# Loads of q and k in half-size transfers and short packets, in a fused window attention and highway layer

## The chip, the core and the metric

The kernel runs on one core of one Trainium2 chip. Five engines work side by side, each through its own instructions in order: PE (TensorE: matmuls, and transposes against an identity matrix), DVE (VectorE), ACT (ScalarE), POOL (GpSimd) and SP (SyncE, which here only issues DMAs). Sixteen DMA engines move data between HBM and the core's SBUF. They take their work from queues: one is fed by POOL, another by SP. The metric is the device time of one execution in microseconds (us), lower is better. The profile is one further execution; its span runs from the first to the last instruction, and the device time of that same execution is a little longer than its span.

## What is computed

```python
B, H, S, D = 8, 8, 576, 64          # q, k, v: [B, H, S, D], float32
scores = scale * q @ k.T            # per batch and head
mask   = (rel >= 0) & (rel < 128)   # rel = query position - key position
attn   = softmax(where(mask, scores - slope[h] * abs(rel), -1e9))
x      = (attn @ v)                 # heads side by side: [4608, 512]
h      = maximum(x @ w_h, 0)
t      = sigmoid(x @ w_t + b_t)
out    = t * h + (1 - t) * x        # [4608, 512], float32
```

Each query sees the 128 keys that end with its own, so that only a band of the scores is worked out. Eight slopes, one for each head, weight the distance.

## The kernel before

**Tiling.** The kernel works on 8 batches. A batch of q or k is 8 heads of 576 positions of 64 numbers. In SBUF it lies as 128 partitions x 2 halves x 1152 bf16: a half is four heads (a = 0 or 1), and a partition holds, for each half, 18 positions of one head, which are 1152 numbers that lie together in HBM: 4608 bytes of float32. The DMA turns float32 into bf16 on its way, so a row arrives as 2304 bytes. The output is worked out in 36 blocks of 128 rows: four to a batch, and one more for each pair of batches from their last 64 rows.

**The steps.** The order of all work is written out by hand as one long string, ORDER; every letter is one step, and each engine gets its instructions in the order of the string. The letters that matter here:

- L, a load, issued by POOL. The list LOADS gives their order: the four halves of q and k of batch 0 into buffers of their own (hq, hk), v of batch 0, the two weight matrices (wH, wT), the bias, then q, k and v of the other batches (lq, lk, va). There are 29 loads: 4 halves, 14 whole q or k, 8 of v and 3 of weights and bias. A v load takes 64 numbers a time, 36 for each partition.
- S, pieces of set-up: on POOL an index (iota, L245) and the identity matrix (ident, L276); on DVE a cast of the index (kq, L253), small operands (kb, ex), 0/1 masks (m, L263 and L265) and their products with the slopes (mk, L268).
- T, a transpose of one half of q or k by DVE into tq or tk (L290), 32 of them. It reads hq, hk, lq or lk.
- s, e, m: scores on PE (L311), their exponential on ACT (p, L326), the mask on DVE (p times mk, both in SBUF, L336).
- V: a copy of half of v's rows to other partitions (vb), by DVE for batches 0 to 2 (L209) and by DMAs of SP for the others (L211).
- p, n: attention times v on PE (L356); DVE divides and writes x (L366, L367).
- x, c, h, r, z, b, a, t: transpose of x on PE against ident (L382), copies and activations on ACT, the two matrix products on PE (L392, L425).
- u, g, o, d: DVE subtracts x (uu, L402 or L404) and multiplies by the gate (uu, L445); the last addition (ot, L450) is done by POOL for 29 of the 36 blocks and by DVE for the others; SP stores the block (L456, L460).

**Buffers.** lq and lk have three buffers each, va and vb four, x eight, uu and ot six each. A load that is issued must find its buffer free.

**What sets the order around the change.** POOL does its loads, its two pieces of set-up and its additions in one sequence. Up to its second addition that is: the four halves, v0, wH, wT, the bias, the index, q1, k1, v1, q3, ident, q2, v2, k2, k3, v3, the first addition, q4, k4, the second addition. The waits are put in by the framework that the kernel is written in, not by the kernel's author.

Of the kernel before, what the change touches and what calls it, by code (L numbers as in the profile page):

```python
# [121 lines left out]
def kernel(  # L122
# [10 lines left out]
    nc = tc.nc  # L133
# [47 lines left out]
    def load(kind, b=0, a=None):  # L181
        if kind in "qk":
            src = (q if kind == "q" else k)[b].rearrange(
                "(a g) (s t) d -> (g s) a (t d)", a=2, t=18)
            if a is None:
                dst = (LQ if kind == "q" else LK)[b % NL]
                nc.gpsimd.dma_start(out=dst[:], in_=src)
            else:
                dst = (HQ if kind == "q" else HK)[a]
                nc.gpsimd.dma_start(out=dst[:], in_=src[:, a])  # L190
        elif kind == "v":
            nc.gpsimd.dma_start(  # L192
                out=VA[b % NV][:, :, 0:D],
                in_=v[b].rearrange("h s d -> (h s) d").rearrange("(c p) d -> p c d", p=P))
        elif kind in "HT":
            i = "HT".index(kind)
            nc.gpsimd.dma_start(
                out=(wH, wT)[i][:],
                in_=(moe_w_h, moe_w_t)[i].rearrange("(c p) n -> p c n", p=P))
        else:  # L200
            nc.gpsimd.dma_start(
                out=bT[0:1, :], in_=moe_b_t.rearrange("(o n) -> o n", o=1))
# [249 lines left out]
    def store(b, s):  # L452
# [5 lines left out]
        for half in range(2):  # L458
            row = (2 * b + half) * S + 512
            nc.sync.dma_start(out=out[row : row + D, :], in_=ot[half * D : (half + 1) * D, :])  # L460

    do = dict(S=setup, L=load, V=move, T=tr, s=scores, e=soft, m=mask, p=pv, n=norm, x=x_tr, c=x_copy, h=mm_h,
              r=relu_act, u=relu_sub, b=bias, B=spread, C=spread_copy, z=mm_z, a=tanh, t=to_gate, g=gate, o=add_x, d=store)
    by = lists()
# [36 lines left out]
```

## Time and profile before

| | us |
|---|---|
| median of three runs | 162.2 |
| lowest and highest of them | 161.84, 163.52 |
| the profiled execution, device time | 161.35 |
| the profiled execution, span | 159.6 |

In the views below, a row of a timeline or of the chain begins with the start in us from the start of the span and the duration in us. A group of instructions has its line, engine, operation, what it writes and reads, its count, and then busy time in us, the mean of one in ns, and the idle time of the engine just before them. "DMA packets" counts what the DMA engines moved in a window, with the size as it is written and GB/s as written. A row of the DMA view for one issue ends with the time from issue to landing in us. The line of 40 digits is the busy share of the DMA engines in 40 equal slices of the span, in tenths.

### The profile page before, as it was taken

The numbers are of one execution on the slowest core, as the hardware profiler recorded it, in microseconds if no ns is written. First come the engines' busy times: TensorE is split into PE (matmuls) and PEld (weight loads), VectorE is DVE, ScalarE is ACT, GpSimd is POOL, SyncE is SP. The second block draws the span as 40 slices with busy tenths as digits, with TensorE's granted clock in tenths as the row PEclk, the third lists the DMA queues.
The fourth block names the chain that finished last, engine by engine and source line by source line (L and its number), as shares of the span: only waits on it lengthen the run. The fifth ranks groups of instructions, "written<-read, shape, count | busy, mean of one in ns | idle before, by whom it ended". The sixth has DMA issues, their size and how long they took to land.

```text
span 159.6 us, 6226 instructions
## 1 busy us (share of the span) xinstructions
PE 131.2 (82%) x2695; PEld 75.3 (47%) x2695; DVE 143.6 (90%) x309; ACT 123.4 (77%) x209; POOL 66.2 (41%) x65
## 2 busy tenths in 40 slices
PE   0003989879998997899999888999999999999940
PEld 0002774345545443555565455555654655656410
DVE  6698879999999999999998999999999999998770
ACT  3001966699878797988989998978989899998740
POOL 7993624562447845422239451354041302210220
PEclk9999999999999999999999999999999999999995
DMA  3999999999999999999999999943103132321333
GB/s 42 193 168 188 209 208 167 201 211 197 250 208 198 253 255 230 214 215 189 252 275 195 178 208 217 282 104 130 66 4 136 68 102 55 116 72 70 131 119 79
DMA packets 48540, 26.55 MB, mean 166 GB/s; under 512 B 38144, under 2 KB 39168, under 8 KB 48512
## 3 DMA queue, kind: packets, MB, share of 16 engines
q0 software_dynamic: 42464, 15.21, 84.2%
q1 hardware_dynamic: 6048, 10.94, 20.3%
q8 instruction: 21, 0.34, 0.9%
q14 instruction: 7, 0.06, 0.1%
HBM read 30.41 MB, written 9.44 MB: 250 GB/s over the span
## 4 chain that ended last, share of the span: by engine, by line
PE 50%; DVE 31%; ACT 8%; issue 5%; DMA 3%; POOL 0%; DVEq 0%; POOLq 0%
PE fs L392 14%; PE fs L425 9%; PE ps L356 9%; PE ps L311 8%; DVE tk L290 6%; DVE x L367 5%; DVE p L336 5%; DVE tq L290 4%; ACT p L326 4%; PE fs L382 3%; DMA hq<-in_q_dram 3%; DVE uu L445 3%; PE ps L425 3%; DVE uu L402 2%; DVE vb L209 2%
## 5 line engine op out<-in xcount | busy, mean ns | idle before, releaser
L450 POOL TENSOR_TENSOR ot<-uu,x 128x512 f32<-128x512 bf16 x29 | 36.0, 1245 | 69.0 <-DVE uu L445 41.1
L326 ACT ACTIVATE p<-ps 128x768 bf16<-128x768 f32 x64 | 49.9, 826 | 7.4 <-PE ps L311 7.4
L311 PE MATMUL ps<-tq,tk 32*64 32x192 bf16 (+2 forms) x1152 | 28.7, 251 | 16.4 <-DVE tk L290 14.3
L336 DVE TENSOR_TENSOR p<-p,mk 128x768 bf16<-128x768 bf16 x64 | 36.4, 590 | 2.1 <-ACT p L326 1.4
L392 PE MATMUL fs<-wH,xt 128*128 128x512 bf16 x140 | 36.1, 381 | 1.7 <-ACT xt L387 1.3
L311 PEld LDWEIGHTS <-tk 32*64 32x64 bf16 x1152 | 20.2, 110 | 24.8 <-DVE tk L290 14.8
L367 DVE TENSOR_TENSOR x<-ps,rd 128x512 bf16<-128x512 f32 x36 | 24.9, 692 | 2.0 <-DVE rd L366 0.5
L425 PE MATMUL fs<-wT,xt 128*128 128x512 bf16 x104 | 26.6, 380 | 0.0
L356 PE MATMUL ps<-va,p 64*128 64x65 bf16 (+1 forms) x544 | 23.5, 194 | 0.9 <-issue 0.4
L356 PEld LDWEIGHTS <-p 64*128 64x128 bf16 (+1 forms) x1088 | 19.1, 98 | 9.9 <-issue 7.1
L433 ACT ACTIVATE tt<-fs 128x512 f16<-128x512 f32 x26 | 15.9, 610 | 7.2 <-PE fs L429 4.8
L356 PE MATMUL ps<-vb,p 64*128 64x65 bf16 (+1 forms) x544 | 21.1, 193 | 0.0
L397 ACT ACTIVATE hh<-fs 128x512 bf16<-128x512 f32 x29 | 17.6, 605 | 3.6 <-PE fs L392 3.3
L425 PEld LDWEIGHTS <-xt 128*128 128x128 bf16 x144 | 12.8, 98 | 14.0 <-issue 0.5
L387 ACT COPY xt<-fs 128x512 bf16<-128x512 bf16 x30 | 17.7, 590 | 1.3 <-PE fs L382 1.2
L392 PEld LDWEIGHTS <-xt 128*128 128x128 bf16 x144 | 11.7, 98 | 14.7 <-ACT xt L387 3.9
L290 DVE STREAM_TRANSPOSE tk<-lk 128x576 uint32<-128x576 uint32 x14 | 17.3, 1246 | 0.0
L290 DVE STREAM_TRANSPOSE tq<-lq 128x576 uint32<-128x576 uint32 x14 | 17.2, 1244 | 0.0
L192 POOL DMA_DIRECT2D va<-in_v_dram x8 | 14.7, 1838 | 5.6 <-DVE p L336 4.8
L438 ACT ACTIVATE tt<-tt 128x512 f16<-128x512 f16 x25 | 16.0, 641 | 0.4
L445 DVE TENSOR_TENSOR uu<-uu,tt 128x512 bf16<-128x512 bf16 x36 | 14.9, 419 | 0.3
L382 PE MATMUL fs<-ident,x 128*128 128x128 bf16 x120 | 12.4, 226 | 3.4 <-DVE x L367 3.0
(55 smaller groups left out, 121.1 us busy)
## 6 DMA issues: line engine op xcount, KB each, us to landing
out_dram<-ot SPq DMA_DIRECT2D x32, 256.0 KB, 4.2
va<-in_v_dram POOLq DMA_DIRECT2D x8, 576.0 KB, 21.1
lq<-in_q_dram POOLq DMA_DIRECT2D x7, 576.0 KB, 20.0
lk<-in_k_dram POOLq DMA_DIRECT2D x7, 576.0 KB, 18.1
vb<-va SPq DMA_DIRECT2D x10, 146.2 KB, 7.0
out_dram<-ot SPq DMA_DIRECT2D x8, 128.0 KB, 4.5
hq<-in_q_dram POOLq DMA_DIRECT2D x2, 288.0 KB, 4.6
hk<-in_k_dram POOLq DMA_DIRECT2D x2, 288.0 KB, 6.3
```

The costliest lines, as they stand in the source:

```text
L290: nc.vector.transpose(out=u32(dst[b % NT][:, a].rearrange("p s e -> p (s e)")).rearrange("p (s t) -> p t s", t=18), in_=u32(src).rearrange ...
L311: nc.tensor.matmul(out=sc[j * D : (j + 1) * D, r, off : off + n * D], lhsT=KT[rows, j, t * D : (t + 1) * D, e], rhs=QT[rows, j, t * D : (t ...
L326: nc.scalar.activation(out=pview(i), in_=SC.pop((b, s, x))[:, :, 0:384].rearrange("p r (g n) -> p r g n", g=2), func=ACTF.Exp, scale=scale)
L336: nc.vector.tensor_tensor(out=p, in0=p, in1=mk, op=ALU.mult)
L356: nc.tensor.matmul(out=av[orow, j, hh * (D + 1) : (hh + 1) * (D + 1)], lhsT=PB[PT[bb, ps, x]][rows, r, lo : lo + orow.stop - orow.start], ...
L367: nc.vector.tensor_tensor(out=x[:], in0=av[:, :, :, 0:D], in1=rd[:].to_broadcast([P, 2, 4, D]), op=ALU.mult)
L387: nc.scalar.copy(out=xt[:], in_=XP.pop(at))
L392: nc.tensor.matmul(out=pa, lhsT=XT[at][:, c * P : (c + 1) * P], rhs=wH[:, c, :], start=c == 0, stop=c == NC - 1)
L397: nc.scalar.activation(out=hh[:], in_=PA.pop(at), func=ACTF.Relu)
L425: nc.tensor.matmul(out=PZ[at], lhsT=xt[:, c * P : (c + 1) * P], rhs=wT[:, c, :], start=own and c == 0, stop=not own and c == NC - 1, skip_ ...
L445: nc.vector.tensor_tensor(out=uu[:], in0=uu[:], in1=TT.pop(at)[:], op=ALU.mult)
L450: eng.tensor_tensor(out=ot[:], in0=UU.pop(at)[:], in1=xf(at), op=ALU.add)
```

## The change

Each whole load of q or k becomes two loads, one for each half of four heads, issued one right after the other from the same place in the order. All q and k loads, the four half loads of batch 0 too, get an upper limit on the length of a packet: 1152 bytes as read, in place of the whole row of 4608, so that a row goes in four packets, each 576 bytes as written. The number of loads grows from 29 to 43. Their order, the buffers, the loads of v and of the weights, and all other steps stay as they are.

```diff
             if a is None:
                 dst = (LQ if kind == "q" else LK)[b % NL]
-                nc.gpsimd.dma_start(out=dst[:], in_=src)
+                for half in range(2):
+                    nc.gpsimd.dma_start(out=dst[:, half], in_=src[:, half],
+                                        max_dma_last_dim=1152)
             else:
                 dst = (HQ if kind == "q" else HK)[a]
-                nc.gpsimd.dma_start(out=dst[:], in_=src[:, a])
+                nc.gpsimd.dma_start(out=dst[:], in_=src[:, a], max_dma_last_dim=1152)
```

## Prediction

> **What bounds the kernel now.** I read the page first, then the chain of work that ended last in its order of time, the timeline of POOL, the DMA view in short windows, and last the timeline of DVE beside POOL's.
>
> ```profile
> span 159.6 us, 6226 instructions
> ...
> PE 131.2 (82%) x2695; PEld 75.3 (47%) x2695; DVE 143.6 (90%) x309; ACT 123.4 (77%) x209; POOL 66.2 (41%) x65
> ...
> DMA  3999999999999999999999999943103132321333
> ...
> L290 DVE STREAM_TRANSPOSE tk<-lk 128x576 uint32<-128x576 uint32 x14 | 17.3, 1246 | 0.0
> L290 DVE STREAM_TRANSPOSE tq<-lq 128x576 uint32<-128x576 uint32 x14 | 17.2, 1244 | 0.0
> ```
>
> The DMA engines are full for two thirds of the span, which looks like a bound, but the last number of the two transpose groups says otherwise: DVE never stood idle for a whole q or k load. What ends last is seen in the chain:
>
> ```profile
> 6.99 1.26 DVE tq L290
> 8.25 0.04 DVE kq L253
> ...
> 8.87 1.17 DVE tk L290
> 10.04 1.21 DVE m L263
> 14.33 0.88 PE ps L311 x29
> ...
> 20.76 0.54 PE fs L382 x4
> ...
> 29.73 0.69 DVE uu L404
> ...
> 67.43 0.40 PE fs L382 x4
> ```
>
> DVE's set-up carries it to 14.33 us, PE and ACT to 29.7, DVE to 67.4, then mostly PE. Between 29.7 and 67.4 a microsecond lost on DVE is close to a microsecond of the kernel.
>
> **The change, part by part.** *POOL's issuing.* All loads are issued by POOL, in order with its own arithmetic:
>
> ```profile
> 1.32 1.25 POOL L190 DMA_DIRECT2D hq<-in_q_dram  x2 [0.81 <-POOLq L485]
> ...
> 3.61 1.86 POOL L192 DMA_DIRECT2D va<-in_v_dram  x1
> 5.42 0.80 POOL L197 DMA_DIRECT2D wH<-in_moe_w_h_dram  x1
> 6.17 0.79 POOL L197 DMA_DIRECT2D wT<-in_moe_w_t_dram  x1
> ...
> 7.52 0.48 POOL L245 IOTA kq_i<- 64x64 int32 x2
> 7.95 0.73 POOL L187 DMA_DIRECT2D lq<-in_q_dram  x1
> ...
> 9.38 1.86 POOL L192 DMA_DIRECT2D va<-in_v_dram  x1
> 11.20 0.73 POOL L187 DMA_DIRECT2D lq<-in_q_dram  x1
> 11.99 0.44 POOL L276 TENSOR_SCALAR_AFFINE_SELECT ident<-ident 128x128 bf16<-128x128 bf16 x1
> 14.72 0.85 POOL L187 DMA_DIRECT2D lq<-in_q_dram  x1 [2.28 <-DMA va<-in_v_dram]
> ```
>
> A transfer of 128 x 4 pieces is what wH and wT are already: one each 0.75 us (5.42 to 6.17). So each of the 14 whole loads costs POOL 2 x 0.75 in place of 0.73, some 0.8 us more, 11 us in all; the four half loads at the start go from 2.29 us together (1.32 to 3.61) to about 3.2 (four of 0.75, the first 0.2 longer as it is now), 0.9 more.
>
> *In flight.* The thirteenth load (14.72) goes into a buffer that nothing has used and yet waits for the fifth, va. So a load waits for the one eight places ahead, and 14 more loads make eight places hold less: a q or k fills two. That, not POOL's 11 us, moves things.
>
> ```profile
> va<-in_v_dram POOLq DMA_DIRECT2D x1, 576.0 KB, 10.8
> wT<-in_moe_w_t_dram POOLq DMA_DIRECT2D x1, 512.0 KB, 12.8
> lq<-in_q_dram POOLq DMA_DIRECT2D x1, 576.0 KB, 15.3
> lk<-in_k_dram POOLq DMA_DIRECT2D x1, 576.0 KB, 25.1
> ```
>
> These are the issues at 3.61, 6.17, 7.95 and 19.28, with the time to landing last: 14.4, 19.0, 23.3 and 44.4 us. The DMA queue always has work, so landings depend on the rate, not on when POOL issued; even so few places hold more than 10 us of transfers. But POOL stands still until a place comes free.
>
> *The rate.* Packets of 576 bytes as written (1152 as read) stand in no row; these windows have the neighbours, 2304, 128 and 1024 bytes:
>
> ```profile
> DMA packets 388, 0.81 MB, mean 202 GB/s; under 512 B 37, under 2 KB 37, under 8 KB 388
> ...
> DMA packets 3646, 0.48 MB, mean 161 GB/s; under 512 B 3628, under 2 KB 3646, under 8 KB 3646
> ...
> DMA packets 621, 0.62 MB, mean 207 GB/s; under 512 B 25, under 2 KB 617, under 8 KB 620
> ```
>
> (5 to 9, 10 to 13 and 15 to 18 us.) On 16 engines a packet starts every 12.7 ns at 128 bytes and every 79 at 1024; halfway is 46 ns, 201 GB/s. A whole load of 590 KB takes 2.92 us at 202 GB/s, 2.93 at 201, 3.66 at 161, 2.85 at 207: from -0.07 to +0.74 us a load, and I take 0, as the near rows are the large ones. There is room for some: k of batch 2 lands at 44.4, its second half is read at 47.0, so 2.6 us. With 2 loads' worth of half loads, q1, k1, q3, q2 and k2 ahead, that is 0.37 us a load.
>
> The Trainium skill, DMA: Bandwidth & Descriptors, How a descriptor splits into AXI transactions, speaks against this: reads go in pieces of 256 bytes from aligned addresses, and 1152 is 4.5 of them, so by it every second packet starts unaligned, and a row takes 152 beats in place of 144. By that a load is estimated at 2.92 x 152/144 = 3.08 us, and the sum would be some 0.3 us higher, from the start alone.
>
> *The start.* POOL's index iota ends 0.9 us later, at 8.9. DVE's cast of it ended at 8.28, right behind tq; now it ends at 9.1, and tk ends at 10.85. On the other side the two m operations, 1.21 us on the chain and now over at 11.25, ended with the v load that POOL was issuing (9.38 + 1.86 = 11.24). That load is now the thirteenth and waits for va's 14.4. m then meets half loads of 0.75 us: free at once it is over at 10.95, held to the end of one at 11.1, of the next at 11.85. So PE's start moves by -0.3 to +0.6 us; I take -0.1. The ident of L276 was ready at 12.43; ahead of it are now both halves of q3, the second waiting for wT: 19.2 with the later first packet, 0.3 from landing to issue (14.4 to 14.72), 0.75, then 0.5 for the select: 20.75, where PE reads it at 20.76. Bound: 0.5 later if the wait is slower. I take +0.1 for both together.
>
> *The adds.* v3, the last load ahead of the first add of POOL (L450), becomes the twenty-third and waits for the second half of q3, at 11.20 + 21.5 = 32.7:
>
> ```profile
> lq<-in_q_dram POOLq DMA_DIRECT2D x1, 576.0 KB, 21.5
> ...
> 27.95 1.41 POOL L450 TENSOR_TENSOR ot<-uu,x 128x512 f32<-128x512 bf16 x1 [2.29 <-DVE uu L445]
> ...
> 32.85 1.33 POOL L450 TENSOR_TENSOR ot<-uu,x 128x512 f32<-128x512 bf16 x1
> ```
>
> So the first add goes to 34.9 us from 27.95. Both halves of q4 and k4 follow; the second half of k4 waits for k2's first half, about 42.9, so the second add goes from 32.85 to about 44. From there POOL catches up, near 60. Buffers do not bite: uu has six, and the first add's is needed by the seventh subtraction at 48.45 (row below). Stores go late with the adds, harmless by the same count.
>
> What the adds do to DVE is the largest term:
>
> ```profile
> 32.70 1.80 DVE L209 COPY vb<-va 64x1170 bf16<-64x1170 bf16 x2
> 34.54 0.56 DVE L336 TENSOR_TENSOR p<-p,mk 128x768 bf16<-128x768 bf16 x1
> ...
> 48.45 0.40 DVE L402 TENSOR_TENSOR uu<-hh,x 128x512 bf16<-128x512 bf16 x1
> ...
> L336 DVE TENSOR_TENSOR p<-p,mk 128x768 bf16<-128x768 bf16 x14 | 9.3, 688 | 0.1
> L402 DVE TENSOR_TENSOR uu<-hh,x 128x512 bf16<-128x512 bf16 x8 | 3.8, 476 | 0.0
> L209 DVE COPY vb<-va 64x1170 bf16<-64x1170 bf16 x4 | 3.3, 834 | 0.1
> ...
> L209 DVE COPY vb<-va x6: 461/464/1305, 14.5 to 50.8; 64x1170 bf16<-64x1170 bf16 x6
> ```
>
> (The groups are DVE's from 30 to 66 us, the last line the copies of the whole run with their shortest, median and longest in ns.) The second copy of 32.70 ends only after the add of 32.85 has (34.18): a DVE operation on two SBUF tiles, or a copy, that starts while an add runs waits for its end. Against 0.56, 0.40 and 0.46 us undisturbed, the groups lose 14 x 0.13 + 8 x 0.08 + 4 x 0.37 = 3.9 us to nine adds, 0.43 each. An add that is not released by the DVE operation ahead of it comes at any moment: of DVE's 63 operations in this stage 36 are of those kinds, they start at 1.75 per us, so an add of 1.25 us catches one in about 7 of 10 cases, with some 0.7 us left: 0.5 each. Ten adds then fall in the stage, o0 among them: 5.0 us, +1.1.
>
> *Nothing else.* DVE's 14 more landings to wait for are all past; PE, ACT and the stores have the same work.
>
> **Sum:** +0.1 start, 0 rate, +1.1 adds: +1.2. On the profiled execution's 161.35 us (span 159.6) that is 162.55; that one was 0.85 under the median of 162.2, so 163.4 us.
>
> **The rivals.** *Hidden:* the late adds catch as much as the punctual ones did ; only the start counts, 162.3 us. For it: POOL has 59% of its time idle. *Faster:* the late adds fall behind transposes, which do not wait. At 0.15 us each that is 10 x 0.15 - 3.9 = -2.4, 159.9 us; it is faster by 1% once the mean is under 0.22 us. Against it: 36 of 63 operations do wait. *Pile-up:* the second to fifth adds queue up on POOL with nothing between them, and DVE loses each time what it loses now without cover, 0.85 us at 32.70 (1.80 for two copies of 0.46): 4 x 0.85 + 6 x 0.5 - 3.9 = +2.5, 164.8 us; it is slower by 1% once the mean of all ten is over 0.54 us. *Slow packets:* at 161 GB/s seven loads bring k2's second half 5.2 us late, 2.6 beyond its room: 163.4 + 2.6 = 166.0 us. Against it: the 1024-byte row is as fast as the large packets. The rule on alignment alone gives 163.7 and lies within the forecast.
>
> **How the numbers follow.** Forecast (162.8 to 164.1) 0.42, hidden 0.20, faster 0.16, pile-up 0.14, slow packets 0.08. The range runs from 160.6, inside the faster case, to 165.6, inside the last two; it leaves out about 0.2. About 1%, 1.6 us, is what a measurement of this kernel can tell from no change. Faster by more: most of the faster case, 0.14. Slower by more, above 163.8: pile-up, slow packets and a quarter of the forecast, 0.14 + 0.08 + 0.11 = 0.33. Within: 0.53.
>
> **What would show it.** POOL's issues of half loads at 0.75 us; the first add near 35 and the second near 44 us; ident near 20.7 and PE's first read of it near 20.9; DVE's m free of the v load; windows of q or k packets near 200 GB/s; the p, uu and vb groups from 30 to 66 us 5 us over undisturbed. I am wrong if loads do not wait for a place (adds on time), if transposes stand idle for lq or lk, or if DVE's loss shrinks.

## The result, and the profile after

| | before | changed |
|---|---|---|
| median of four runs each, us | 162.02 | 166.94 |
| lowest and highest | 161.60, 163.52 | 166.72, 167.21 |
| the profiled execution, device time and span | 161.35, 159.6 | 166.89, 165.1 |

The changed kernel takes 1.029 times as long [1.022, 1.036]: 4.9 us more, where the forecast was 163.4 us and the range ended at 165.6. Ratios here and below leave disturbed runs out, so one can stand beside a quotient of medians that differs from it. Lines of the changed kernel from the load on have numbers higher by 2.

From the page of the changed kernel:

```profile
span 165.1 us, 6245 instructions
...
PE 133.3 (81%) x2695; PEld 76.4 (46%) x2695; DVE 146.8 (89%) x309; ACT 123.7 (75%) x209; POOL 77.2 (47%) x79
...
PEclk9999999999975999999999999999999999999997
```

POOL has 11.0 us more, near the forecast (11 for the whole loads and 0.9 for the four at the start). DVE has the same 309 instructions and 3.2 us more. New is the pair of digits 7 and 5 in the TensorE clock near 50 us.

POOL's timeline and DVE's, after:

```profile
21.32 0.45 POOL L278 TENSOR_SCALAR_AFFINE_SELECT ident<-ident 128x128 bf16<-128x128 bf16 x1
...
36.34 1.22 POOL L452 TENSOR_TENSOR ot<-uu,x 128x512 f32<-128x512 bf16 x1
37.52 1.55 POOL L188 DMA_DIRECT2D lq<-in_q_dram  x2
42.09 1.48 POOL L188 DMA_DIRECT2D lk<-in_k_dram  x2 [3.02 <-DMA va<-in_v_dram]
43.58 3.38 POOL L452 TENSOR_TENSOR ot<-uu,x 128x512 f32<-128x512 bf16 x3
...
55.68 1.17 POOL L452 TENSOR_TENSOR ot<-uu,x 128x512 f32<-128x512 bf16 x1
```

```profile
19.15 0.69 DVE L369 TENSOR_TENSOR x<-ps,rd 128x512 bf16<-128x512 f32 x1
...
43.36 3.90 DVE L404 TENSOR_TENSOR uu<-hh,x 128x512 bf16<-128x512 bf16 x1
...
55.40 1.88 DVE L338 TENSOR_TENSOR p<-p,mk 128x768 bf16<-128x768 bf16 x1 [0.66 <-ACT p L328]
```

The first addition comes at 36.34 us, the next three together at 43.58, one behind the other (x3, 3.38 us). DVE's subtraction at 43.36 starts in the record 0.22 us ahead of them (the DVE operation before it ended at 43.52), while POOL was still issuing the load of k4, and ended after the third: 3.90 us for an operation of 0.42. Set side by side, operation by operation, DVE stands 0.1 us behind the kernel before at 43 us, 3.7 behind after this one operation, 5.4 behind after the one at 55.40, and 5.5 at the end. DVE's groups of 30 to 66 us, which are to be read against those of the prediction:

```profile
L338 DVE TENSOR_TENSOR p<-p,mk 128x768 bf16<-128x768 bf16 x13 | 11.0, 874 | 0.7 <-ACT p L328 0.7
L404 DVE TENSOR_TENSOR uu<-hh,x 128x512 bf16<-128x512 bf16 x6 | 6.0, 995 | 0.3 <-ACT hh L399 0.3
...
L211 DVE COPY vb<-va 64x1170 bf16<-64x1170 bf16 x4 | 1.9, 484 | 0.1
```

A mean of 874 ns was 688, one of 995 was 476. One sum is used below for every run, DVE's *excess*: over the whole trace, the time of DVE's masks, subtractions and multiplications on two SBUF tiles, scalings of tt and copies of v above their undisturbed 0.55, 0.42, 0.29 and 0.46 us, where it is above them by more than 0.04. It was 5.5 us before and is 10.2 after; the 4.8 between them is the size of the loss. It is read from one trace of each kernel and does not follow the time in every run below.

PE waits for x meanwhile, and then its clock is halved. Windows of before, then of after, and PE's waits after:

```profile
44.00:48.00 4.00, 3.76 (x50) 2.00 (x48) 4.00 (x7) 3.30 (x6) 1.53 (x2) 1.00 1.73 207
48.00:54.00 6.00, 4.86 (x132) 2.65 (x129) 5.86 (x13) 5.45 (x10) 4.53 (x4) 1.00 1.54 216
```

```profile
44.00:48.00 4.00, 1.29 (x6) 0.39 (x4) 3.97 (x3) 1.71 (x3) 4.00 (x5) 0.92 2.04 173
48.00:54.00 6.00, 5.84 (x56) 2.67 (x64) 5.64 (x12) 1.78 (x4) 2.37 (x3) 0.50 1.54 243
```

```profile
PE fs L384 <- DVE x L369: 5.3, 4, 2.9
```

(A window's row has its length, then busy time and count of PE, PEld, DVE, ACT and POOL, then the granted clock.) PE stood for 2.9 us, and the granted clock was 0.50 from 47.4 to 54.2, while PE was busy for 5.84 of 6 us. This lies on the chain of the changed kernel, which runs on PE from 48.16 us and comes back to DVE with the mask at 55.40:

```profile
48.16 0.61 PE fs L384 x4
...
49.94 1.82 PE fs L394 x4
51.76 1.71 PE fs L427 x4
...
54.56 0.82 ACT p L328
```

DVE was free for that mask at 54.74, waited 0.66 us for ACT and so met the addition of 55.68: the step from 3.4 to 5.4 us behind. At full clock eight such matmuls take 1.83 us (rows of another run, further down), here 3.53. That the mask would otherwise have been over before that addition is worked out from these times; no run shows it.

### The profile page after: what moved, and what is told of

Read it like the earlier page. It is cut to its first block, busy times and chain, and to the rows that moved or that the text cites. A ratio compares the mean times of both kernels' runs of the same rounds, so it can differ in the third digit from the quotient of the medians.

```text
span 165.1 us, 6245 instructions
## 1 busy us (share of the span) xinstructions
PE 133.3 (81%) x2695; PEld 76.4 (46%) x2695; DVE 146.8 (89%) x309; ACT 123.7 (75%) x209; POOL 77.2 (47%) x79
## 4 chain that ended last, share of the span: by engine, by line
PE 36%; DVE 35%; DMA 11%; issue 6%; POOL 5%; ACT 4%; DVEq 0%; POOLq 0%
PE fs L394 11%; DVE p L338 9%; DMA wT<-in_moe_w_t_dram 8%; PE fs L427 7%; PE ps L358 6%; DVE x L369 6%; DVE tq L292 5%; DVE uu L404 4%; PE ps L313 4%; DVE uu L447 3%; DVE tk L292 3%; PE fs L384 3%; PE ps L427 3%; DMA out_dram<-ot 3%; ACT p L328 2%
## 5 line engine op out<-in xcount | busy, mean ns | idle before, releaser
L452 POOL TENSOR_TENSOR ot<-uu,x 128x512 f32<-128x512 bf16 x29 | 35.3, 1223 | 58.7 <-DVE uu L447 31.6
L313 PE MATMUL ps<-tq,tk 32*64 32x192 bf16 (+2 forms) x1152 | 29.2, 249 | 16.3 <-DVE tk L292 14.3
L338 DVE TENSOR_TENSOR p<-p,mk 128x768 bf16<-128x768 bf16 x64 | 38.5, 628 | 2.3 <-ACT p L328 2.1
L394 PE MATMUL fs<-wH,xt 128*128 128x512 bf16 x140 | 36.9, 388 | 1.6 <-ACT xt L389 1.1
L427 PE MATMUL fs<-wT,xt 128*128 128x512 bf16 x104 | 27.5, 390 | 0.0
L358 PE MATMUL ps<-va,p 64*128 64x65 bf16 (+1 forms) x544 | 24.0, 196 | 0.5 <-ACT p L328 0.4
L358 PE MATMUL ps<-vb,p 64*128 64x65 bf16 (+1 forms) x544 | 21.6, 194 | 0.0
L188 POOL DMA_DIRECT2D lk<-in_k_dram x14 | 10.8, 775 | 15.0 <-DMA va<-in_v_dram 7.4
L404 DVE TENSOR_TENSOR uu<-hh,x 128x512 bf16<-128x512 bf16 x30 | 16.7, 556 | 0.4 <-ACT hh L399 0.3
```

The costliest lines, as they stand in the source:

```text
L313: nc.tensor.matmul(out=sc[j * D : (j + 1) * D, r, off : off + n * D], lhsT=KT[rows, j, t * D : (t + 1) * D, e], rhs=QT[rows, j, t * D : (t ...
L338: nc.vector.tensor_tensor(out=p, in0=p, in1=mk, op=ALU.mult)
L358: nc.tensor.matmul(out=av[orow, j, hh * (D + 1) : (hh + 1) * (D + 1)], lhsT=PB[PT[bb, ps, x]][rows, r, lo : lo + orow.stop - orow.start], ...
L394: nc.tensor.matmul(out=pa, lhsT=XT[at][:, c * P : (c + 1) * P], rhs=wH[:, c, :], start=c == 0, stop=c == NC - 1)
L404: nc.vector.tensor_tensor(out=uu[:], in0=HH.pop(at)[:], in1=xf(at), op=ALU.subtract)
L427: nc.tensor.matmul(out=PZ[at], lhsT=xt[:, c * P : (c + 1) * P], rhs=wT[:, c, :], start=own and c == 0, stop=not own and c == NC - 1, skip_ ...
```

## Experiments

In the diffs a step is named by its letter and its number, counted from 0: o1 is the second addition, L18 the load of k4, g1 the multiplication whose result o1 adds. "moved(ORDER, 'o', 4, 'ahead', 'o', 4)" takes the fifth addition out of ORDER and puts it ahead of the next one.

### Is it the places in flight or the short packets?

Halves as in the change, rows whole:

```diff
-                    nc.gpsimd.dma_start(out=dst[:, half], in_=src[:, half],
-                                        max_dma_last_dim=1152)
+                    nc.gpsimd.dma_start(out=dst[:, half], in_=src[:, half])
...
-                nc.gpsimd.dma_start(out=dst[:], in_=src[:, a], max_dma_last_dim=1152)
+                nc.gpsimd.dma_start(out=dst[:], in_=src[:, a])
```

> The change with its two transfers for each q and k load, but whole rows of 4608 bytes as packets. Theory A (loads in flight: each load waits for the one eight places ahead, the additions of POOL come late and in a row, and DVE waits through the row): the loads are 43 as in the change, so most of the loss stays: the second addition of POOL starts at 41 to 45 us in place of 32.85, some DVE operation from 40 to 60 us lasts over 2 us, time 1.015 to 1.035 of the kernel before. Rival B (short packets cost the time): no more than 1.008.

Measured: 164.73 us, ratio 1.014 [1.006, 1.022]. The second, third and fourth addition again run in a row, and this time a mask waits through it:

```profile
41.45 3.91 DVE L337 TENSOR_TENSOR p<-p,mk 128x768 bf16<-128x768 bf16 x1
```

The other way round, the kernel before with its whole loads in long packets, and one load of 64 numbers, which nobody reads, behind each of the 14, so that the places are used up as in the change:

```diff
                 nc.gpsimd.dma_start(out=dst[:], in_=src)
+                nc.gpsimd.dma_start(out=EXTRA.pop()[0:1, :], in_=(q if kind == "q" else k)[b, 0, 0:1, :])
```

> The kernel before with its whole loads and long packets; behind each of the 14 whole q and k loads goes one more load of 64 numbers that nobody reads. Theory A: it takes places in flight as the halves of the change do, and almost no DMA time: first addition at 32 us or later in place of 28.0, second at 40 us or later in place of 32.9, time 1.01 to 1.035 of the kernel before. Rival B (short packets, or the halves themselves): 0.997 to 1.006. The sign of the place theory rests on the additions' start times more than on the time, as the phase at which late additions meet DVE is open.

Measured: 168.01 us, the median of four runs between 165.33 and 168.25, too far apart for a ratio. Additions at 35.0, 43.5, 44.6 and 45.7 us, and the subtraction waits through three:

```profile
43.89 3.23 DVE L404 TENSOR_TENSOR uu<-hh,x 128x512 bf16<-128x512 bf16 x1
```

So the places alone make the row, without one short packet. But halves in long packets cost 2.8 us (164.73 - 161.90, the median of before beside it), not 4.9: about half of the loss is not told by this.

### What does a row of additions cost?

The kernel before, its loads untouched, with the fourth and fifth addition put right ahead of the sixth:

```diff
+ORDER = moved(ORDER, "o", 4, "ahead", "o", 4)
+ORDER = moved(ORDER, "o", 3, "ahead", "o", 3)
+ORDER = moved(ORDER, "d", 4, "ahead", "d", 4)
+ORDER = moved(ORDER, "d", 3, "ahead", "d", 3)
```

> The kernel before with its old loads; only the fourth and fifth additions of POOL, and their stores, are put off until just ahead of the sixth, so that POOL does three in a row from about 49.3 us. Theory A: the copies of vb that start at 49.7 wait to the end of the row at about 52.8, 2.3 us later than now, and the time goes to 1.009 to 1.018 of the kernel before. Rival D (late additions in a row are harmless to DVE, the loss of the change lies in its loads): 0.997 to 1.004.

And with the fifth alone put there (the first and third of these lines):

> The kernel before, with the fifth addition put right ahead of the sixth, so that two run one behind the other near 49.5 us (three cost one copy 3.29 us, a single one 0.64). Theory A (one DVE operation waits through the whole row): the copy of v or the mask that is issued while they run lasts 2 to 2.5 us, one operation alone. The rival (a row only makes more single meetings, each with its own operation): no DVE operation lasts over 1.9 us.

Measured: 165.74 us and 1.023 [1.017, 1.029] for three; 164.79 us in one run for two. DVE's timeline of before, of two in a row, of three in a row, at the same copy of v:

```profile
49.72 1.10 DVE L209 COPY vb<-va 64x1170 bf16<-64x1170 bf16 x1
```

```profile
49.72 2.20 DVE L221 COPY vb<-va 64x1170 bf16<-64x1170 bf16 x1
```

```profile
49.98 3.29 DVE L223 COPY vb<-va 64x1170 bf16<-64x1170 bf16 x1
```

One, two, three additions: 1.10, 2.20, 3.29 us. Each further addition in the row adds its whole 1.1 us to the same operation of DVE; there is no gap in which DVE gets in. The row of three, on loads that nothing was done to, costs 3.8 us, more than the expectation's 1.018 allowed. Not all of it is the row. The copy right behind, 0.46 us in before, took 1.69 us in the run of two and here 1.72:

```profile
53.28 1.72 DVE L223 COPY vb<-va 64x1170 bf16<-64x1170 bf16 x1
```

No addition runs beside it, but the issue of a v load, which stands behind the row on POOL and ended 0.26 us ahead of the copy. Set side by side with before, DVE falls back by 2.2 us with the first copy and by another 1.25 with the second (1.1 and 1.2 in the run of two).

### The change without its row

Six loads moved behind the additions that they held up:

```diff
+ORDER = moved(ORDER, "L", 20, "behind", "o", 5)
+ORDER = moved(ORDER, "L", 19, "behind", "o", 4)
+ORDER = moved(ORDER, "L", 18, "behind", "o", 3)
+ORDER = moved(ORDER, "L", 17, "behind", "o", 3)
+ORDER = moved(ORDER, "L", 16, "behind", "o", 2)
+ORDER = moved(ORDER, "L", 15, "behind", "o", 0)
```

> The whole change, with short packets and 43 loads, but in POOL's order k of batch 3, v of batch 3, q and k of batch 4, q and k of batch 5 stand behind the additions that they stood ahead of. Theory A: the additions start within 2 us of the kernel before (28.0, 32.9, 35.5, 40.7, 46.1), no DVE operation lasts over 1.6 us, and the loss goes: 0.995 to 1.012 of the kernel before. Rival B (short packets) and rival C (POOL's additional issuing, 11 us): 1.02 to 1.035, as the packets and the issuing are all still there.

Measured: 165.41 us (163.74 to 166.57), 1.012 [1.005, 1.019]. No row is left and no DVE operation lasts over 1.6 us; the excess is 7.4. That is at the edge of what theory A allowed (0.995 to 1.012): better than the change, 1.029 [1.022, 1.036], but not back at before.

Before asking further, theory A's other side: if waits for additions are lost time, the kernel before should gain from avoiding the four that it has (0.84, 0.96, 0.64 and 0.96 us).

```diff
+ORDER = moved(ORDER, "g", 1, "ahead", "n", 3)
+ORDER = moved(ORDER, "o", 1, "ahead", "L", 18)
+ORDER = moved(ORDER, "g", 2, "behind", "u", 3)
+ORDER = moved(ORDER, "o", 2, "behind", "n", 4)
+ORDER = moved(ORDER, "d", 2, "behind", "p", 5)
+ORDER = moved(ORDER, "o", 5, "ahead", "L", 20)
+ORDER = moved(ORDER, "g", 6, "ahead", "T", 12)
+ORDER = moved(ORDER, "o", 6, "behind", "T", 12)
```

> The kernel before, with four additions moved so that each runs beside transposes or DVE operations on PSUM, not beside copies or masks: the second ahead of k4's load with its gate ahead of the division, the third's gate behind the seventh mask and subtraction, the sixth ahead of k5's load, the seventh's gate ahead of the transpose. Theory A says that what an addition costs is the wait of a DVE operation on two SBUF tiles, and the four cost 0.84, 0.96, 0.64 and 0.96 us in before's trace, 3.4 us of DVE together: the operations over their undisturbed time sum to 5.5 us in before and should fall to 2 to 3 us; the time falls by 1 to 3 us, to 159 to 161. The rival, that DVE's waits are absorbed by PE and ACT in this stage (so that the 4.8 us which DVE lost under the change were not its price), gives before's time within 0.7 us although the waits are gone.

Measured: 160.96 us, 0.995 [0.993, 0.998]. The excess falls to 3.7 (2 to 3 were expected) and DVE is 0.7 us ahead from 57 to 84 us, but level again at 86.6, where both kernels come out of the issue of a v load. This gain on DVE was kept in part, up to the next thing that did not move; the change's loss stood at 5.5 us at the end.

Now both sets of moves on the change, for the additions that are still in the way (g1, g2, o2, d2, g6 and o6 of the last list, and the six loads), with short packets and with long:

> The whole change, with the loads of batches 3 to 5 moved behind the additions that they held up (as in the run with the loads moved alone: 163.74 and 164.39 us where it was undisturbed), and with the second, third and seventh additions placed beside transposes and DVE operations on PSUM. Theory A (what is lost is DVE's waiting for additions): DVE's operations over their undisturbed time sum to 5 us or less, and the time comes within 1 us of before, 161 to 163. The rival (besides the additions, the change costs something of its own, packets or landings): the waits fall as well, but the time stays above 163.5.

> The run above with the rows of 4608 bytes kept whole: halves, loads behind the additions, additions beside transposes, no short packets. The difference between the two runs is what the short packets cost by themselves, with no row of additions in the way. Theory A with the packets at no price (as predicted): within 0.7 us of each other. The rival, that the short packets cost some 1 us through later landings at the start (first landings of the second to fourth half load 1.2 to 1.3 us later): this run is 0.7 to 1.5 us faster.

| no row | median, us | ratio to before | excess, us |
|---|---|---|---|
| short packets | 166.16 | 1.022 [1.013, 1.031] | 5.7 |
| long packets | 161.71 | 0.997 [0.992, 1.002] | 4.5 |

This is where theory A falls short. With the row gone and DVE's excess back at that of before, the kernel with short packets is still 2.2% slower, and the packets alone are worth 4.45 us, 2.5% by the ratios. Of this, 1.2 us can still be DVE's waits (5.7 against 4.5). Halves in long packets, without the row, cost nothing.

### Where do the short packets cost?

Short packets on the four half loads of the kernel before, all else as it was:

```diff
-                nc.gpsimd.dma_start(out=dst[:], in_=src[:, a])
+                nc.gpsimd.dma_start(out=dst[:], in_=src[:, a], max_dma_last_dim=1152)
```

> The kernel before, with the short packets on the four half loads of batch 0 alone; the whole loads and so the places in flight are as before. Theory A (late additions in a row on POOL are the loss): the additions stand where they stood, from 27.95 and 32.85 us, and the time is that of before, within 0.7 us (the four half loads cost POOL 0.9 us more at the start, which before absorbs by 38 us). Theory B (the packets of 576 bytes themselves cost time): four of the change's thirty-two half loads are short, all of them at the start where each microsecond of a late landing goes on to PE; hk1 lands about 1.3 us later, and the time is 1 us or more above before, 163 or more.

Measured: 162.68 us, 1.004 [1.000, 1.007]. That lies between the two theories. DVE is 1.2 us late from the start to 86 us in the trace and 1.9 at the end: the half loads land late, and m still meets the v load's issue, so nothing pays it back.

Packets of half the length on the whole change, max_dma_last_dim=576 in both places:

> The whole change, but every q and k packet half as long again, 576 bytes as read and 288 as written: the suspected cost of short packets doubled, the places in flight as in the change. Theory A: landings and so the additions move only as far as the rate falls; by the rows of 128 bytes (161 GB/s) and 576 (199) the rate is between, about 180 GB/s, a batch's load 0.3 us later, the additions in a row near 44 to 46 us, and the time that of the change, 166 to 168 us. Theory B (the packets are the cost): the loss over before at least doubles, from 4.9 to 8 us or more, 170 us or more, with gaps of DVE before the transposes of lq and lk.

Measured: 168.88 us, 1.044 [1.037, 1.051]: 7.3 us over before (161.62 beside it) against 4.9 for the change. More than theory A allowed, less than the 8 of theory B; a subtraction waits 4.29 us through the row.

Then the two groups of half loads apart, in the schedule without the row: short packets on the 28 later ones only, and on the four at the start only.

> Halves, loads behind the additions, additions beside transposes, as in the two runs at 166.16 (all packets short) and 161.71 us (none); here the four half loads of batch 0 keep long packets and the other 28 half loads have short ones. Theory S (the short packets act on the start: the second to fourth half load land 1.2 to 2.2 us later, DVE is 1.4 us behind, PE waits longer for DVE and its clock is halved for it): near the run without short packets, 161 to 163 us. Theory L (they act on the later landings: v of batch 4 lands 4.2 us later, and so on): near the run with all, 165 us or more.

> The same schedule with short packets on the four half loads of batch 0 alone. Theory S: near the run with all packets short, 164.5 us or more. Theory L: near the run with none, 161 to 163 us.

| short packets on | median, us | ratio to before |
|---|---|---|
| none | 161.71 | 0.997 [0.992, 1.002] |
| the four at the start | 163.26 | 1.007 [1.002, 1.011] |
| the 28 others | 163.98 | 1.011 [1.007, 1.016] |
| all 32 | 166.16 | 1.022 [1.013, 1.031] |

Neither theory alone: 1.0% by the four, 1.4% by the 28, and the sum of 2.4% is near what all of them cost (2.5%), with intervals of half a per cent and more. The first x that DVE writes shows the part of the four. Long at the start (no short packets; then the 28 short), then short at the start (the four; then all):

```profile
18.35 0.69 DVE L390 TENSOR_TENSOR x<-ps,rd 128x512 bf16<-128x512 f32 x1
```

```profile
17.81 0.69 DVE L391 TENSOR_TENSOR x<-ps,rd 128x512 bf16<-128x512 f32 x1
```

```profile
19.53 0.69 DVE L390 TENSOR_TENSOR x<-ps,rd 128x512 bf16<-128x512 f32 x1
```

```profile
19.88 0.69 DVE L391 TENSOR_TENSOR x<-ps,rd 128x512 bf16<-128x512 f32 x1
```

In before it was 19.19, in the change 19.15. Halves would bring the first x 0.8 to 1.4 us forward, because m no longer meets the issue of a v load; the short packets take 1.2 to 2.1 away again. The rate is the smaller part of this: in the change the four half loads land at 6.13, 8.16, 9.65 and 11.14 us, in before at 5.53, 6.97, 8.41 and 9.85. The last two follow at 1.49 in place of 1.44, and 1.2 of the delay is there when the second lands; why is open.

The same two groups in the change's own order, with the row:

> The change itself, in its own order, but the four half loads of batch 0 keep long packets. The row of three additions stays. With all packets long this order took 164.73 us, with all short 166.94. Theory S: 164 to 165.5, near the first. Theory L: 166.3 or more. A third way: the row's loss depends on where DVE stands when the additions begin, so that the start's 1 us only moves it, and the time is anywhere between 164 and 168 with the wait through the row still one operation of 3.3 to 4.3 us.

> The change's order in halves, short packets on the four half loads of batch 0 alone. Theory S: near the change, 166 us or more. Theory L: near 164.73. In both, one DVE operation waits through the row of three additions, near 43 us.

Measured: 164.82 us (163.88 to 167.96), 1.015 [1.004, 1.026], and 166.10 us (162.82 to 167.83), 1.010 [0.995, 1.026]. Four runs each, too far apart to place either between the halves with long packets (1.014) and the change (1.029). In the first a subtraction waits 3.58 us through the row. In the second the row is there as well, from 41.78 us, but DVE is in two transposes until 43.9 and the subtraction behind them waits 1.72 us, against the expectation; this trace is of a run of 162.82 us. It is the expectation's third way, a row whose price hangs on what DVE does when it begins.

For the 28, POOL's issuing or the transfers? POOL's groups without short packets and with all short, count 14 each, the mean in ns:

```profile
L210 POOL DMA_DIRECT2D lk<-in_k_dram x14 | 7.7, 553 | 8.3 <-DVE rd L389 3.9 <-DMA va<-in_v_dram 3.0 <-DMA hk<-in_k_dram 1.3
```

```profile
L210 POOL DMA_DIRECT2D lk<-in_k_dram x14 | 10.6, 764 | 9.7 <-DMA va<-in_v_dram 4.5 <-DVE rd L390 3.9 <-DMA hk<-in_k_dram 1.2
```

A half load in short packets takes 0.76 us to issue, in long ones 0.55: 28 x 0.21 = 5.9 us of POOL. So long packets with more work on POOL, and packets between the two lengths (max_dma_last_dim=2304):

```diff
                     nc.gpsimd.dma_start(out=dst[:, half], in_=src[:, half])
+                    for _ in range(6):
+                        nc.gpsimd.memset(PAD[:], 0.0)
```

> Halves, long packets, loads behind the additions, additions beside transposes (161.71 us), with six memsets of one column on POOL behind each of the 28 half loads of the later batches, which at about 0.035 us each (as the four at the start of before's trace follow each other) give POOL the 0.21 us that a half load in short packets takes longer to issue. Theory P (POOL's longer issuing is the price of the 28): near 164, as with 28 short half loads. Theory D (the transfers' later landings are): within 0.8 us of 161.71.

> The schedule without the row, every q and k packet 2304 bytes as read, between the 1152 of 166.16 us and the 4608 of 161.71. If the cost goes with the number of packets (four, two or one to a row) it is a third of the way, about 163.2; if it comes from a threshold between 1152 and 4608 it is at one end, under 162.2 or over 165.5.

Measured: 167.72 us, 1.031 [1.021, 1.041], and 164.18 us, 1.012 [1.008, 1.016]. The first missed its dose: the six memsets took 0.9 us and more each time, not 0.21 (17.4 us busy in all and 8.1 idle between them), so that POOL had some 25 us more, and the kernel lost 3.4%; DVE's excess rose from 4.5 to 8.8. It shows that POOL's time is not free, with all transfers as they were; in proportion 5.9 us would be 0.8% of the 1.4, but nothing shows that it goes in proportion. The second is at neither end and not at a third, but a little over half of the way, with 0.73 us to issue a half load; its excess of 6.7 is above that of both ends, so that waits of DVE are in it that are not the packets' own. How the cost of the 28 divides between POOL and the transfers stays open.

### Faster than before

SP's copies of v of batches 4 and 5 ahead of the stores that they waited behind, on top of the four moved additions:

```diff
+ORDER = moved(ORDER, "V", 4, "ahead", "d", 11)
+ORDER = moved(ORDER, "V", 5, "ahead", "d", 12)
```

> The kernel before with the four moved additions, and with SP's copies of v of batches 4 and 5 put ahead of the stores that they wait behind. With the four moved additions alone DVE was 1.06 us ahead until 84 us, and that was gone by 86.6: PE made no use of it at 80 us, where it waits for the copies of v (issued at 74.7, behind a store that waits for an addition, though v had landed at 72.1). If that copy is the next bound, it is issued at 72.2 and the time falls by another 0.5 to 1 us, to about 160.2. If another landing or ACT bounds it there, the time stays at 160.96 within 0.5.

Measured: 161.30 us, 0.996 [0.992, 1.000]. The first copies were issued at 72.8 us in place of 74.7 and nothing came of it: DVE again comes out of the v load's issue at 86.4.

On top of that, the load of v1 behind the masks:

```diff
+        nc.gpsimd.tensor_tensor(out=AFTER_MK[:], in0=MK[:, 0, 320:384], in1=MK[:, 1, 320:384], op=ALU.add)
...
+ORDER = moved(ORDER, "S", 6, "ahead", "L", 10)
+ORDER = moved(ORDER, "L", 10, "behind", "S", 5)
```

> The run above, and at the start the load of v of batch 1 held back by a small addition on POOL that reads the finished masks, so that the two operations that make m (1.21 us on before's chain, ended by that load's issue at 11.24) meet no issue. It adds one small POOL addition whose output nobody reads. By theory A's reading of the start m takes 0.2 us instead of 1.3, PE starts 1 us earlier than 14.33, and the time falls by 0.3 to 0.8 us if nothing else (v of batch 0 lands at 14.43) takes its place; the rival is that the landing does, and the time is that of the run above within 0.3.

Measured: 160.41 us, 0.987 [0.979, 0.995], the fastest of all kernels here. m takes 0.18 us in place of 1.36, and DVE is 1.0 us ahead from 23 to 30 us:

```profile
10.18 0.18 DVE L286 TENSOR_SCALAR m<-kq 128x64 bf16<-128x64 f32 x1
```

It keeps the whole loads in long packets: the gain that the change's halves had at the start, without their price.

## Why the prediction was wrong, step by step

The sum was +1.2 us, the change cost 4.9. The direction and the late additions were right; the price of the additions and that of the packets were not.

- **Issuing and places in flight: right.** Half loads took 0.77 us (0.75 forecast), the fifteenth load waited for the seventh, wT, at 20.53, the first addition came at 36.34 (34.9), the second at 43.58 (44), and no transpose waited for a late q or k beyond the start.
- **The start, +0.1: right as a sum, by luck.** PE started at 14.29 against 14.33 and the first x came at 19.15 against 19.19; m was free of the v load. The two parts, the half loads' delay and m's gain, were each over 1 us and cancel. The ident was wrong: it ended at 21.77, not 20.75, half a microsecond beyond its bound, as wT landed at 20.24 in place of 19.2. PE stood 1.36 us for it and had made that up by 23.8.
- **The additions, +1.1: the step that failed first, in its size.** "An add of 1.25 us catches one in about 7 of 10 cases, with some 0.7 us left: 0.5 each" prices additions one by one. From 30 to 66 us the groups p, uu and vb were to be 5.0 us over undisturbed; by the rows above they were 13 x 0.31 + 6 x 0.60 + 4 x 0.02 = 7.7, with eight additions there and not ten. DVE's excess over the whole trace rose by 4.8 us. The two largest pieces are 3.5 in one operation behind three additions and 1.3 in another at 55.40. The pile-up rival named the mechanism and gave it 0.14, but took 0.85 for each addition of the queue, what one costs before; the runs with one, two and three in a row show 1.1 each, all on the same operation.
- **"Nothing else": failed for PE.** Its work was the same, its clock was not: 0.50 for 6.8 us behind the row, on the chain, with DVE 0.66 us waiting at its end. The sum had no term for it.
- **The rate, 0: near in itself, wrong as the price of the packets.** Windows of 5 to 9 and of 20 to 23 us after, with almost only packets of 576 bytes as written:

```profile
DMA packets 1333, 0.74 MB, mean 186 GB/s; under 512 B 40, under 2 KB 1333, under 8 KB 1333
...
DMA packets 1041, 0.60 MB, mean 199 GB/s; under 512 B 31, under 2 KB 1040, under 8 KB 1040
```

The forecast had 201 GB/s, and 202 for long packets. That is 1 to 8% less, and the 5.6% that the rule of the Trainium skill asked for (DMA: Bandwidth & Descriptors, How a descriptor splits into AXI transactions) lies between. What failed is the step from the rate to "0" for the packets, and "That, not POOL's 11 us, moves things". With the row gone, short packets cost 2.5%: 1.0% through the four half loads at the start, 1.4% through the 28 others, whose issuing takes 5.9 of those 11 us. In the change itself their share is the distance from 1.014 to 1.029.
- **The two causes are not a sum.** With long packets, clearing the row (and placing additions better, which gave before 0.5%) brings 1.014 to 0.997. With short ones it brings 1.029 to 1.012 in the one kernel and 1.022 in the other, whose intervals overlap. Taking away one of the causes leaves from 40% to three quarters of the loss, taking away both leaves none. Why they overlap was not shown.
- **The rivals.** *Faster* did not come true: the late additions did not meet transposes by chance; placed there on purpose, in the kernel before, they gained 0.5%. Nor did *hidden*. *Slow packets* was wrong in its mechanism, the rate, and near in its sum (166.0) by luck.

## What to carry to other kernels

Before splitting transfers, count what else stands in the issuing engine's sequence: here eight loads fit in flight, each half load takes a place and more time to issue, and what is queued behind comes late and together. Price work that comes together as one block against one operation of the engine that waits for it, here DVE, not one by one at random, and look what that engine does when the block begins. And a rate as good as before does not make short packets free: look at the first transfers, which something waits for, and at the issuing time of each.

## What the runs showed of the hardware

**DVE gets no turn between queued additions.** The subtraction of 43.36 us starts in the record before the first of the three additions and ended after the last. With packets of half the length the subtraction of 45.41 us stands 0.64 us ahead of the first addition, in the issue of a half load, and ended after the third as well (4.29 us). The Trainium skill, SBUF — State Buffer, Who interferes with whom, says that whoever issues first of the two holds the shared ports and the other waits for that instruction (it says so of DVE's two-port modes, and that an operation with two inputs in SBUF contends too); here the one whose record starts first, while POOL was issuing a DMA, waited through three instructions.

**In these runs a PE that stood for 2.1 us or more got half its clock.** Over the 20 traces, before their last 9 us, PE stood for over 1 us 43 times. After all 12 stands of 2.1 us or more the granted clock fell to 0.50, within 7 us of their start, for 3.41 us or twice that; after 8 of the 14 between 1.4 and 2.0; after none of the 17 shorter ones. Two more falls had no single stand of 1 us ahead. The Trainium skill, TensorE: Matmul & The Clock Gate, What's actually happening, has a free-running window of about 3.4 us and a fall after an idle window: the lengths agree, but stands far shorter than a window sufficed. In the change this lies on the chain from 48.16 us (above). It does elsewhere too: of short packets without the row, where the fall of 97.9 us is one of the two without such a stand, then of long,

```profile
97.94 1.89 PE fs L416 x4
99.82 1.67 PE fs L449 x4
```

```profile
96.19 0.97 PE fs L415 x4
97.16 0.86 PE fs L448 x4
```

the same eight matmuls took 3.56 us where they took 1.83. In the schedule without the row the clock lost in the median run, span times one minus the granted share, rises with the short packets: 3.1 us with none, 3.4 with the four, 3.9 with the 28, 5.1 with all; before, 1.3. How much of the packets' price goes this way was not separated.

**Beside the issue of a v load, DVE's copies and scalings wait, its masks mostly do not.** Over the 20 traces, with no addition running as they started, all 5 copies of v that started in such an issue ended 0.26 to 0.27 us behind it, after 1.69 to 1.87 us, and all 27 scalings of tt ended 0.09 to 0.12 us behind it; m was held for 1.2 us in before. Of 79 masks that started there 73 took their usual time, among them those from 16.83 us in the change, and 6 were held, one at 35.04 us in the change for 1.0 (1.52 in all). What decides for those 6 is not settled.
